# Four edits to a one-core attention and mixture-of-experts kernel: the last stores, one small sum, a weight fetch and a gate

## The chip, the core and the metric

The kernel runs on one core of one Trainium2 chip. A core has five engines that work at the same time, each through its own list of instructions in order: TensorE (PE, matrix products; its weight loads are shown as PEld), VectorE (DVE), ScalarE (ACT), GpSimd (POOL) and SyncE (SP, which here only issues transfers). Transfers run on 16 DMA engines and are issued from the lists of SP, ACT and POOL. The metric is the device time of one execution in microseconds (us). Before the change it is 377.31 us, the median of three runs (376.6 to 377.85).

## The reference: what is computed

Two stages follow each other. The first is grouped attention over 8 batches of 384 rows, with 16 query heads and 4 key/value heads of 64 columns:

```
scores = scale * np.matmul(q, k.transpose(0, 1, 3, 2))
scores = scores - np.max(scores, axis=-1, keepdims=True)
attn = np.exp(scores)
attn = attn / (np.sum(attn, axis=-1, keepdims=True) + 1e-09)
return np.matmul(attn, v)
```

Its output, 3072 rows of 1024 columns, goes through a two-level gate: softmax over 4 groups, then softmax over 4 experts of the best group. Each row goes through its one best expert and is scaled by the product of both gate weights:

```
h = np.maximum(xg[mask_e] @ w1[g, e], 0.0)
ye = h @ w2[g, e]
out[tok_idx] = combined[:, None] * ye
```

All inputs and the output are 32-bit floats. `w1` and `w2` of an expert are 1024 x 1024 each.

## The kernel before

**Staging.** The kernel works batch by batch. One attention batch has 24 units (4 key/value heads by 6 blocks of 64 keys). In unit u PE computes the scores of unit u+2 (line 308) and the product of unit u with the values (line 327), ACT takes the exponential (314), POOL adds the exponentials of two units together (`pair`, 335) and DVE sums that pair along the keys (`reduce`, 344). At the end of a batch DVE joins the partial sums (`join_keys`, 397), PE adds them over the partitions (`sums`, 405), DVE takes the reciprocal (414) and, for four parts m = 0 to 3, spreads it (421) and multiplies the attention output with it (`normalise`, 425). ACT or POOL cast the result to 16 bits (`cast`).

**Experts.** For each batch the kernel guesses one expert that its rows are likely to choose (from the mean of the values, `guess_mean`, line 446 on PE and 448 on DVE), fetches that expert's two matrices (`pick_w1`, 512, and `pick_w2`, 518, two transfers from POOL's list), and runs the expert for all rows of the batch: `moe_h` (602 on PE, ReLU on ACT at 606 and 609) and `moe_y` (616 on PE, scaling by the gate weight on ACT at 635, stores from SP at 637). A loop at the end of the program would take what no guess covered; with this input its count is zero, and the core only reads that count (916) and branches over the loop (918).

**Order.** The program is written out in the order in which each engine runs it; there is no scheduler. The expert of batch f runs in `block(f + 1)`, between the attention of batch f+1 and that of batch f+2; the expert of batch 0 runs in the last units of batch 1's attention and in `first_block`. The steps between units of batch 1 stand in the table `steps1`: an entry `22: [first_fetch]` runs after the 22nd unit's pair and reductions. `first_fetch` puts three things in POOL's list: a one-element copy that waits for the transposes of the next batch's queries (`after_transposes`, 570), and the fetches of batch 1's `w1` and `w2`. The pair of unit 23, the last, comes after it.

**Gate.** `gate_softmax` is a row of small DVE operations (471 to 491) with one exponential on ACT (497) and a few more on DVE (499 to 503); `out_weights` ends it (580, 584). Each batch's gate runs in its own block, except batch 1's: its logits come early in the attention of batch 2, and its softmax runs in `block(2)`.

**Constants.** At the start `gate_matrix_1` transposes the gate weights on PE into a PSUM tile, copies them to SBUF (233) and adds neighbouring blocks into `wgs` (236). A PE product with `wgs` follows (241).

**The last stores.** The last batch's output is made in three chunks of 128 rows by `last_y`. A chunk's 128 partitions belong to two groups of 64 rows of the output (`halves`). Chunks 0 and 1 are stored with one transfer for each group and half of the columns (904). The third chunk is made in three pieces of 512, 384 and 128 columns, and each piece is stored with one transfer that covers both groups (900): its leading dimension has 2 entries, the next one 64.

Of the kernel before, what the change touches and what calls it, by code (L numbers as in the profile page):

```python
# [18 lines left out]
def kernel(  # L19
# [11 lines left out]
    nc = tc.nc  # L31
    P = 128
    B, Hq, S, D = q.shape
    _, Hkv, _, _ = k.shape
    SC = S // P
# [190 lines left out]
    def gate_matrix_1(which):  # L226
        state["gm"] = pt = ps_tile(which, [P, 2, 512])
        pe = pt[:, 0, :Eg * 5 * KQ].rearrange("p (e n) -> p e n", e=Eg)
        wv = wraw.rearrange("a (p e) -> a e p", e=Eg)
        for e in range(Eg):  # L230
            nc.tensor.transpose(out=pe[:, e], in_=wv[:, e, :],
                                identity=id128f[:5 * KQ, :5 * KQ])
        nc.vector.tensor_copy(
            out=wg[:, :, :NW].rearrange("p k (a e) -> p e a k", e=Eg),
            in_=pe.rearrange("p e (a k) -> p e a k", k=KQ))
        nc.vector.tensor_add(out=wgs, in0=wg[:, 0::2, :NW], in1=wg[:, 1::2, :NW])

    def gate_matrix_2():
        pt = state["gm"]
# [152 lines left out]
    def join_keys(b, g0, g1):  # L392
        if b not in red:
            red[b] = gpool.tile([P, Hkv, 2, NB], F32, name="red", bufs=2)
        same = len(set(parts[b][g0:g1])) == 1
        for g, h in [(g0, g1)] if same else [(g, g + 1) for g in range(g0, g1)]:
            nc.vector.tensor_reduce(
                out=red[b][:, g:h].rearrange("p g t j -> p g (t j)"),
                in_=red3[b][:, g:h, :parts[b][g]].rearrange("p g c t j -> p g (t j) c"),
                axis=AX.X, op=ALU.add)  # L400
# [65 lines left out]
    def gate_softmax(b, gl, guessed):  # L466
        lo, hi = 0, SC + 1 if guessed else SC
        n, nt = hi, SC
        gl = gl[:, lo:hi]
        mx = gpool.tile([P, 2, SC + 1], F32, name="mx")[:, :, lo:hi]  # L470
        nc.vector.tensor_reduce(out=mx[:, 0, :], in_=gl[:, :, :G], axis=AX.X, op=ALU.max)
        sh = gpool.tile([P, 2, SC + 1, G], F32, name="sh")[:, :, lo:hi]
        nc.vector.tensor_tensor(out=sh[:, 0], in0=gl[:, :, :G],
                                in1=mx[:, 0, :].unsqueeze(2).to_broadcast([P, n, G]),
                                op=ALU.subtract)
        ohg = gpool.tile([P, SC + 1, G], F32, name="ohg")[:, lo:hi]
        nc.vector.tensor_single_scalar(ohg, sh[:, 0], 0.0, op=ALU.is_ge)
        pr = gpool.tile([P, SC + 1, G, Eg], F32, name="pr")[:, lo:hi]
        nc.vector.tensor_tensor(out=pr, in0=gl[:, :, G:NW].rearrange("p c (g e) -> p c g e", g=G),
                                in1=ohg.unsqueeze(3).to_broadcast([P, n, G, Eg]), op=ALU.mult)  # L480
        el = gpool.tile([P, SC + 1, Eg], F32, name="el")[:, lo:hi]
        nc.vector.tensor_reduce(out=el, in_=pr.rearrange("p c g e -> p c e g"), axis=AX.X,
                                op=ALU.add)
        nc.vector.tensor_reduce(out=mx[:, 1, :], in_=el, axis=AX.X, op=ALU.max)
        nc.vector.tensor_tensor(out=sh[:, 1], in0=el,
                                in1=mx[:, 1, :].unsqueeze(2).to_broadcast([P, n, Eg]),
                                op=ALU.subtract)
        ohe = gpool.tile([P, SC + 1, Eg], F32, name="ohe")[:, lo:hi]
        nc.vector.tensor_single_scalar(ohe, sh[:, 1], 0.0, op=ALU.is_ge)
        oh = oh_all[:, b, lo:hi]  # L490
        nc.vector.tensor_tensor(out=oh.rearrange("p c (g e) -> p c g e", g=G),
                                in0=ohg.unsqueeze(3).to_broadcast([P, n, G, Eg]),
                                in1=ohe.unsqueeze(2).to_broadcast([P, n, G, Eg]), op=ALU.mult)

        def weights():
            ex = gpool.tile([P, 2, SC, G], F32, name="ex")
            nc.scalar.activation(ex, sh[:, :, :nt], ACT.Exp)
            sm = gpool.tile([P, 2, SC], F32, name="smx")
            nc.vector.tensor_reduce(out=sm, in_=ex, axis=AX.X, op=ALU.add)
            wt = gpool.tile([P, SC], F32, name="wt")  # L500
            nc.vector.tensor_mul(out=wt, in0=sm[:, 0, :], in1=sm[:, 1, :])
            nc.vector.reciprocal(out=wt, in_=wt)
            nc.vector.tensor_tensor(out=cw_all[:, b], in0=oh_all[:, b, :SC],
                                    in1=wt.unsqueeze(2).to_broadcast([P, SC, NE]), op=ALU.mult)
        return weights
# [72 lines left out]
    def out_weights(b):  # L578
        m = gpool.tile([P, SC, NE], F32, name="m")
        nc.vector.tensor_tensor(out=m, in0=cw_all[:, b],  # L580
                                in1=oh1_all[:, b, :].unsqueeze(1).to_broadcast([P, SC, NE]),
                                op=ALU.mult)
        we = gpool.tile([P, SC], F32, name="we", bufs=2)
        nc.vector.tensor_reduce(out=we, in_=m, axis=AX.X, op=ALU.add)
        weff[b] = we
# [3 lines left out]
    def out_rows(o):  # L589
        return o.rearrange("(p x) d -> x p d", x=NC)  # L590

    def halves(c):

        for h in range(2):
            j = 2 * c + h
            yield slice(h * H2, (h + 1) * H2), 2 * (j % SC) + j // SC
# [26 lines left out]
    def moe_h(b, f0, which):  # L623
        if f0 == 0:
            hTs[b] = xpool.tile([P, FQ, S], BF16, name="hT", bufs=1)
        ffn_h(xb[b], w1s[b], hTs[b], f0, which)
# [97 lines left out]
    def first_fetch():  # L724
# [33 lines left out]
            do(moe_h, 0, 6, "s"),  # L758
        ],
        18: [do(before_attention, 1)],  # L760
        22: [first_fetch],
    }
    at[1].run(steps1)

# [41 lines left out]
    def block(b):  # L806
        last = b == B - 1
        f = b - 1
        if b + 2 < B:
            load_v(b + 2)  # L810
        if not last:
            after_transposes(b + 1)
        pick_w1(b)
        pick_w2(b)
        if not last:
            sum_v(b + 1)
        if b + 2 < B:
            load_k(b + 2)
            load_q(b + 2)
        moe_h(f, 0, "s")  # L820
        at[b].reduce(NU - 1)
        join_keys(b, 0, Hkv)
        moe_h(f, 2, "s")
        sums(b, 0, Hkv, "o")
        normalise(b, 0)
        normalise(b, 1)
        moe_h(f, 4, "s")
        normalise(b, 2)
        moe_h(f, 6, "s")
        cast(b, 0)  # L830
        cast(b, 1)
        if b == 2:
            gate_softmax(1, state["gl"], False)()
            out_weights(1)
        normalise(b, 3)
        moe_y(f, 0, "s")
        cast(b, 2)
        pt = ps_tile("o")
        y = ffn_y(w2s[f], hTs[f], 1, "s", (0,))
        vm = None if last else guess_mean(b + 1, pt)  # L840
        ffn_y(w2s[f], hTs[f], 1, "s", (1,), y)
        cast(b, 3)
        y_out(f, 1, y)
        gate_logits(b, pt)
        if not last:
            guess_logits(vm, guess_out(pt))
            at[b + 1] = Attn(b + 1)
            at[b + 1].score(0)
            at[b + 1].score(1)
        w = gate_softmax(b, gate_rows(pt, not last), not last)  # L850
        if not last:
            pick(b + 1)
            pick_index(b + 1)
            read_pick(b + 1)
        w()
        out_weights(b)
        y = ffn_y(w2s[f], hTs[f], 2, "o")
        if last:
            y_out(f, 2, y)
            return {}  # L860
        return {1: [do(y_out, f, 2, y, True)]}
# [25 lines left out]
    def last_y(i, c, c0, n):  # L887
        y = ps_tile("so"[i % 2])[:, 0, :n]
        for f in range(FQ):
            nc.tensor.matmul(out=y, lhsT=hTs[B - 1][:, f, c * P:(c + 1) * P],  # L890
                             rhs=w2s[B - 1][:, f, c0:c0 + n], start=(f == 0), stop=(f == FQ - 1))
        o, w = ots[c][:, c0:c0 + n], weff[B - 1][:, c:c + 1]
        if i % 2 == 0:
            nc.vector.tensor_scalar(o, y, w, None, op0=ALU.mult)
        else:
            nc.scalar.mul(o, y, w)
        rows_ = out_rows(out[(B - 1) * S:])
        if c + 1 == SC:
            xs = [x for _, x in halves(c)]
            (nc.scalar if HALF < c0 + n < DM else nc.sync).dma_start(  # L900
                out=rows_[xs[0]:xs[1] + 1:xs[1] - xs[0], :, c0:c0 + n], in_=o)
            return
        for ps, x in halves(c):
            nc.sync.dma_start(out=rows_[x][:, c0:c0 + n], in_=o[ps])

    ots = {}
    i = 0
# [107 lines left out]
```

## Time and profile before

| | us |
|---|---|
| median of three runs | 377.31 (376.6 to 377.85) |
| the profiled execution's own time | 379.33 |
| its span, from first to last instruction | 377.1 |
| PE busy | 353.9 (94%) |
| DVE, ACT, POOL busy | 245.3, 224.3, 221.5 (65%, 59%, 59%) |
| mean granted TensorE clock, as a share of full speed | 0.983 |

The profiled execution carries 2.2 us that lie outside its span. A row of the profile's views names an engine, a line, the operation, the tile it writes, an arrow and the tiles it reads; a number in square brackets at its end is the time for which the engine stood idle before it, and what released it. The lists of instructions are in order, but their times overlap between engines, so an engine's idle time costs something only where another one is waiting for it in turn. The chain of work that ended last is PE for 83% of the span; DVE follows with 6%.

### The profile page before, as it was taken

What the parts mean: (1) busy time and instruction counts of PE and PEld (TensorE: products, weight loads), DVE (VectorE), ACT (ScalarE), POOL (GpSimd) and SP (SyncE); (2) the same over time, 40 slices, a digit from 0 to 9 for tenths busy, and PEclk for the clock granted to TensorE, in tenths of its full rate; (3) what the DMA queues carried; (4) which work ended last, traced back from release to release, by engine and by line L of the source; (5) the groups of instructions that cost most, each with busy time, mean ns of one, the idle gap of its engine ahead of it and who ended that gap; (6) DMA issues with size and microseconds to landing.
All of it is one profiled execution on the core that took longest, in us unless ns stands there. A gap on an engine that the chain in (4) does not pass through costs nothing.

```text
span 377.1 us, 9174 instructions
## 1 busy us (share of the span) xinstructions
PE 353.9 (94%) x3823; PEld 185.9 (49%) x3823; DVE 245.3 (65%) x462; ACT 224.3 (59%) x296; POOL 221.5 (59%) x175
## 2 busy tenths in 40 slices
PE   7899999699999999999999999999999999999940
PEld 3445555335554555654455544654555554655520
DVE  5587669476779676857678566857678566851310
ACT  4699845259924795367925596367935596263210
POOL 8789885739963299606991199606990199300000
PEclk9999999989999999999999999999999999999995
DMA  8959999699989999999969999799959960799231
GB/s 197 203 116 166 227 170 156 117 249 250 175 157 203 233 218 196 179 207 246 192 136 209 244 199 206 135 207 248 184 107 206 247 145 2 121 205 276 56 93 37
DMA packets 69395, 67.14 MB, mean 178 GB/s; under 512 B 37054, under 2 KB 49598, under 8 KB 69350
## 3 DMA queue, kind: packets, MB, share of 16 engines
q0 software_dynamic: 26640, 41.03, 63.0%
q1 hardware_dynamic: 42228, 24.81, 29.0%
q8 instruction: 32, 0.52, 0.5%
q10 hardware_dynamic: 482, 0.67, 0.5%
q14 instruction: 13, 0.11, 0.1%
HBM read 86.07 MB, written 12.58 MB: 262 GB/s over the span
## 4 chain that ended last, share of the span: by engine, by line
PE 83%; DVE 6%; ACT 3%; POOL 2%; issue 2%; POOLq 0%; ACTq 0%
PE ps_o L327 29%; PE ps_s L602 19%; PE ps_s L616 10%; PE ps_s L308 8%; PE ps_o L616 7%; PE ps_o L440 3%; ACT e L314 2%; PE ps_s L890 1%; POOL e L335 1%; PE ps_o L405 1%; PE ps_o L602 1%; PE ps_o L890 1%; DVE xT L425 1%; DVE e L421 1%; PE ps_o L268 1%
## 5 line engine op out<-in xcount | busy, mean ns | idle before, releaser
L335 POOL TENSOR_TENSOR e<-e 128x768 f32<-128x768 f32 x91 | 162.8, 1820 | 84.9 <-PE ps_s L308 78.1
L314 ACT ACTIVATE e<-ps_s 128x768 f32<-128x768 f32 x187 | 147.4, 812 | 23.8 <-PE ps_s L308 21.4
L327 PE MATMUL ps_o<-e,v_raw 64*64 64x384 f32 x1496 | 149.1, 482 | 0.1
L344 DVE TRANSPOSE_TENSOR_REDUCE red<-e 128x24 f32<-128x768 f32 x95 | 91.5, 972 | 41.5 <-POOL e L335 41.4
L602 PE MATMUL ps_s<-xb,w 128*128 128x384 bf16 x480 | 80.9, 326 | 0.1
L327 PEld LDWEIGHTS ps_o<-e,v_raw 64*64 64x64 f32 x1496 | 54.3, 133 | 36.8 <-issue 28.9
L602 PEld LDWEIGHTS <-w 128*128 128x128 bf16 x512 | 49.5, 98 | 35.7 <-issue 4.5
L308 PE MATMUL ps_s<-qT,kT 64*64 64x384 bf16 x768 | 63.8, 326 | 1.2 <-ACT e L314 0.7
L616 PEld LDWEIGHTS <-hT 128*128 128x128 bf16 x336 | 32.2, 99 | 39.6 <-issue 3.8
L606 ACT ACTIVATE hT<-ps_s 128x768 bf16<-128x768 f32 x23 | 18.6, 810 | 55.7 <-PE ps_s L602 52.3
L616 PE MATMUL ps_s<-w,hT 128*128 128x512 bf16 x224 | 50.9, 385 | 0.0
L308 PEld LDWEIGHTS <-kT 64*64 64x64 bf16 x768 | 24.1, 105 | 36.4 <-issue 34.0
L635 ACT ACTIVATE ot<-ps_s,we 128x1024 f32<-128x1024 f32 x14 | 15.6, 1113 | 21.9 <-PE ps_s L616 20.4
L616 PE MATMUL ps_o<-w,hT 128*128 128x512 bf16 x112 | 25.6, 380 | 0.0
L369 DVE COPY xT<-ps_o 128x768 f32<-128x768 f32 x26 | 24.0, 923 | 2.0 <-PE ps_o L327 1.4
L421 DVE STREAM_TRANSPOSE e<-inv 128x768 f32<-128x768 f32 x26 | 25.2, 971 | 0.2
L425 DVE TENSOR_TENSOR xT<-xT,e 128x768 f32<-128x768 f32 x24 | 23.6, 981 | 0.8
L430 ACT CAST xb<-xT 128x768 bf16<-128x768 f32 x28 | 22.2, 833 | 0.0
L414 DVE RECIPROCAL inv<-ps_o 64x96 f32<-64x96 f32 (+2 forms) x20 | 12.7, 635 | 9.4 <-PE ps_o L405 9.2
L461 DVE STREAM_TRANSPOSE gl<-ps_o 128x96 f32<-128x96 f32 x8 | 2.3, 283 | 21.7 <-PE ps_o L453 16.1
L609 ACT ACTIVATE hT<-ps_s 128x384 bf16<-128x384 f32 x14 | 6.1, 488 | 12.5 <-PE ps_s L602 12.5
L440 PE MATMUL ps_o<-xT,wg 128*32 128x96 f32 x448 | 10.7, 248 | 0.9 <-DVE vm L448 0.9
(133 smaller groups left out, 221.5 us busy)
## 6 DMA issues: line engine op xcount, KB each, us to landing
w<-in_moe_w_dram POOLq DMA_DIRECT2D x16, 2048.0 KB, 20.7
out_dram<-ot SPq DMA_DIRECT2D x43, 256.0 KB, 6.9
q_raw<-in_q_dram POOLq DMA_DIRECT2D x7, 768.0 KB, 27.5
v_raw<-in_v_dram SPq DMA_DIRECT2D x7, 384.0 KB, 5.4
k_raw<-in_k_dram POOLq DMA_DIRECT2D x7, 192.0 KB, 24.2
out_dram<-ot SPq DMA_DIRECT2D x8, 128.0 KB, 2.4
w<-in_q_dram POOLq DMA_DIRECT2D x3, 192.0 KB, 6.6
w<-in_k_dram SPq DMA_DIRECT2D x2, 192.0 KB, 3.7
```

The costliest lines, as they stand in the source:

```text
L308: nc.tensor.matmul(out=sT[r * H2:(r + 1) * H2, s, :S], lhsT=kT[b][s * D:(s + 1) * D, key_block(b, s, g // 2, c), ks], rhs=qT[b][s * D:(s + ...
L314: nc.scalar.activation(e.rearrange("p t (s x) -> p s t x", s=2), sT[:, :, :S].rearrange("p s (t x) -> p s t x", t=2), ACT.Exp, scale=scale)
L327: nc.tensor.matmul(out=oT[t * D:(t + 1) * D, r, :S], lhsT=vraw[b][r * H2:(r + 1) * H2, g // 2, c * D:(c + 1) * D], rhs=self.e[u][r * H2:(r ...
L335: nc.gpsimd.tensor_add(out=self.e[u - 1], in0=self.e[u - 1], in1=self.e[u])
L344: nc.vector.tensor_reduce(out=red3[b][:, g, parts[b][g]].rearrange("p t j -> p (t j)"), in_=self.e[w].rearrange("p t (j x) -> p (t j) x", ...
L369: nc.vector.tensor_copy(out=dst, in_=src)
L421: nc.vector.transpose(out=rb.rearrange("p k (j x) -> p k j x", x=32), in_=inv[b][:, ks].unsqueeze(3).to_broadcast([P, 2, NB, 32]))
L425: eng.tensor_mul(out=x, in0=x, in1=rb)
L430: nc.scalar.copy(out=xb[b][:, ks, :], in_=xT[b][:, ks, :])
L440: nc.tensor.matmul(out=pt[32 * t:32 * t + 32, 0, :S // 4], lhsT=wg[:, head_pair(m), :], rhs=x[:, t], start=(m == 0), stop=(m == KQ - 1))
L602: nc.tensor.matmul(out=h[:, jj, :S], lhsT=w1[:, head_pair(m), (f0 + jj) * P:(f0 + jj + 1) * P], rhs=x[:, m, :], start=(m == 0), stop=(m == ...
L616: nc.tensor.matmul(out=y[:, nh, :], lhsT=hT[:, f, c * P:(c + 1) * P], rhs=w2[:, f, nh * HALF:(nh + 1) * HALF], start=(f == 0), stop=(f == ...
```

## The change

Four places are edited.

1. The column sum in `gate_matrix_1` reads its second operand from the PSUM tile instead of from the copy in SBUF.
2. `first_fetch` moves from step 22 of batch 1 to step 23.
3. Batch 1's `gate_softmax` and `out_weights` move, within `block(2)`, from behind the second cast to the place behind `join_keys`, before the second part of `moe_h`.
4. Each piece of the third last chunk is stored with two transfers of 64 rows. For the pieces of 384 and of 128 columns the second one is issued from ACT's list.

```diff
@@ gate_matrix_1
-        nc.vector.tensor_add(out=wgs, in0=wg[:, 0::2, :NW], in1=wg[:, 1::2, :NW])
+        nc.vector.tensor_add(out=wgs.rearrange("p g (a e) -> p g a e", e=Eg),
+                             in0=wg[:, 0::2, :NW].rearrange("p g (a e) -> p g a e", e=Eg),
+                             in1=pe.rearrange("p e (a k) -> p k a e", k=KQ)[:, 1::2])
@@ steps1
-        22: [first_fetch],
+        23: [first_fetch],
@@ block
         at[b].reduce(NU - 1)
         join_keys(b, 0, Hkv)
+        if b == 2:
+            gate_softmax(1, state["gl"], False)()
+            out_weights(1)
         moe_h(f, 2, "s")
...
         cast(b, 1)
-        if b == 2:
-            gate_softmax(1, state["gl"], False)()
-            out_weights(1)
         normalise(b, 3)
@@ last_y
-        rows_ = out_rows(out[(B - 1) * S:])
-        if c + 1 == SC:
-            xs = [x for _, x in halves(c)]
-            (nc.scalar if HALF < c0 + n < DM else nc.sync).dma_start(
-                out=rows_[xs[0]:xs[1] + 1:xs[1] - xs[0], :, c0:c0 + n], in_=o)
-            return
-        for ps, x in halves(c):
-            nc.sync.dma_start(out=rows_[x][:, c0:c0 + n], in_=o[ps])
+        engs = (nc.sync, nc.scalar) if HALF < c0 + n and c + 1 == SC else (nc.sync, nc.sync)
+        for eng, (ps, x) in zip(engs, halves(c)):
+            eng.dma_start(out=out_rows(out[(B - 1) * S:])[x][:, c0:c0 + n], in_=ots[c][ps, c0:c0 + n])
```

Line numbers of the changed kernel are 2 higher than before from the column sum on, and 3 lower behind `last_y`.

The stores at the end of SP's list before (64x512 are the two earlier chunks, the leading 2 is the pair of row groups):

```order
L904 DMA out_dram<-ot 64x512 x8
L900 DMA out_dram<-ot 2x64x512
L900 DMA out_dram<-ot 2x64x128
```

and in SP's list now:

```order
L901 DMA out_dram<-ot 64x512 x10
L901 DMA out_dram<-ot 64x384
L901 DMA out_dram<-ot 64x128
```

ACT's list ended with one store of 2x64x384; it ends now with two:

```order
L901 DMA out_dram<-ot 64x384
L901 DMA out_dram<-ot 64x128
```

Three transfers have become six, four on SP and two on ACT, and none has a leading 2.

POOL's list at the end of batch 1's attention, before (`e` are the exponentials, `tok` the one-element copy, `w_1052` and `w_1054` batch 1's expert matrices):

```order
L335 TENSOR_TENSOR e<-e 128x768 x3
L570 COPY tok<-qT 1x1
L512 ISA
L512 DMA w_1052<-in_moe_w_dram 128x8x1024
L518 ISA
L518 DMA w_1054<-in_moe_w_dram 128x8x1024
L335 TENSOR_TENSOR e<-e 128x768
L112 TENSOR_TENSOR vs<-v_raw 128x384
```

and now:

```order
L337 TENSOR_TENSOR e<-e 128x768 x4
L572 COPY tok<-qT 1x1
L514 ISA
L514 DMA w_1059<-in_moe_w_dram 128x8x1024
L520 ISA
L520 DMA w_1061<-in_moe_w_dram 128x8x1024
L112 TENSOR_TENSOR vs<-v_raw 128x384
```

The fourth pair, that of unit 23, stands ahead of the copy and the two fetches.

DVE's list in `block(2)` from the join of the key sums on, now (the first 3 and the last 2 of the 15 operations of batch 1's gate stand here; before, all 15 stood behind the third `L425`, ahead of the fourth `L421`):

```order
L399 TENSOR_REDUCE red<-red_1248 128x96
L473 TENSOR_REDUCE mx<-gl 128x3
L475 TENSOR_TENSOR sh<-gl,mx 128x12
L479 TENSOR_SCALAR ohg<-sh 128x12
...
L582 TENSOR_TENSOR m<-cw_all,oh_all 128x48
L586 TENSOR_REDUCE we<-m 128x3
L416 RECIPROCAL inv<-ps_o_1612 64x2x4x12 x2
L423 STREAM_TRANSPOSE e<-inv 128x768
L427 TENSOR_TENSOR xT<-xT,e 128x768
```

The reciprocal of batch 2's sums, and with it the whole normalising, stands behind the gate. On ACT the gate's exponential moves with it, from behind the casts to a place between the first and the second ReLU of this block.

## Rows read from the trace of the kernel before

**Rows 1.** Waits of PE: line waited for, us in total, times, longest.

```profile
PE ps_o L405 <- DVE red L397: 2.9, 1, 2.9
PE ps_o L241 <- DVE wgs L236: 1.3, 1, 1.3
PE ps_o L440 <- DVE vm L448: 0.9, 1, 0.9
```

**Rows 2.** Stretches at the end: length, busy times, then PEclk, DMA share, GB/s.

```profile
361.00:362.00 1.00, 1.00 (x8) 0.61 (x7) 0.68 (x1) 0.00 (x0) 0.00 (x0) 1.00 0.86 201
366.00:374.00 8.00, 0.00 (x0) 0.00 (x0) 0.00 (x0) 0.00 (x0) 0.00 (x0) 0.61 0.13 50
```

**Rows 3.** Stores of lines 904 and 900: ns min/median/max to issue, first and last start.

```profile
L904 SPq DMA_DIRECT2D out_dram<-ot x8: 466/534/591, 355.1 to 360.4; - x8
DMA to landing us min/median/max: 2.2/2.4/2.4
...
L900 SPq DMA_DIRECT2D out_dram<-ot x2: 518/570/622, 361.7 to 363.0; - x2
```

**Rows 4.** Line 918, the branch at the end, same columns.

```profile
L918 SPq EVENT_SEMAPHORE  x9: 17/17/17, 364.1 to 375.4; - x9
...
L918 ACTq EVENT_SEMAPHORE  x1: 17/17/17, 366.3 to 366.3; - x1
```

**Rows 5.** Order of time, 9 to 28 us: start, us, engine, line, operation.

```profile
9.84 1.81 POOL L335 TENSOR_TENSOR e<-e 128x768 f32<-128x768 f32 x1
10.13 1.61 DVE L236 TENSOR_TENSOR wgs<-wg 128x80 f32<-128x80 f32 x1
...
25.67 0.95 DVE L425 TENSOR_TENSOR w<-w,ps_o 128x768 f32<-128x768 f32 x1
25.80 1.83 POOL L335 TENSOR_TENSOR e<-e 128x768 f32<-128x768 f32 x1 [0.52 <-PE ps_s L308]
```

**Rows 6.** Order of time, end of batch 1's attention, 60 to 75 us.

```profile
61.56 5.39 POOL L335 TENSOR_TENSOR e<-e 128x768 f32<-128x768 f32 x3 [4.40 <-PE ps_s L602]
62.28 3.06 ACT L314 ACTIVATE e<-ps_s 128x768 f32<-128x768 f32 x4
66.29 5.35 PE L616 MATMUL ps_s<-w,hT 128*128 128x512 bf16 x24
68.59 0.18 POOL L570 COPY tok<-qT 1x1 bf16<-1x1 bf16 x1 [1.64 <-DMA qT<-q_raw]
...
70.99 1.82 POOL L335 TENSOR_TENSOR e<-e 128x768 f32<-128x768 f32 x1
72.84 0.98 DVE L344 TRANSPOSE_TENSOR_REDUCE red<-e 128x24 f32<-128x768 f32 x1 [4.30 <-POOL e L335]
```

**Rows 7.** The chain that ended last, 74 to 81 us: start, us, what.

```profile
74.57 1.17 PE ps_o L405 x4
75.74 2.76 PE ps_s L616 x8
78.50 1.73 PE ps_o L616 x8
```

**Rows 8.** One stretch, columns as in rows 2.

```profile
74.50:76.00 1.50, 1.43 (x6) 1.14 (x7) 0.24 (x2) 0.00 (x0) 1.44 (x3) 0.50 0.92 171
```

**Rows 9.** Order of time, block 2, 108 to 122 us.

```profile
110.08 0.18 POOL L570 COPY tok<-qT 1x1 bf16<-1x1 bf16 x1 [2.74 <-DMA qT<-q_raw]
110.26 1.52 DVE L414 RECIPROCAL inv<-ps_o 64x96 f32<-64x96 f32 x2 [1.40 <-PE ps_o L405]
...
114.74 0.45 POOL L114 TENSOR_TENSOR vsum<-vs 128x128 bf16<-128x128 f32 x1
...
118.02 0.16 DVE L471 TENSOR_REDUCE mx<-gl 128x3 f32<-128x12 f32 x1
...
120.44 0.17 PE L446 MATMUL ps_o<-halfb,vsum 128*128 128x2 bf16 x1
...
121.09 0.97 DVE L421 STREAM_TRANSPOSE e<-inv 128x768 f32<-128x768 f32 x1
```

## What was predicted

> **What bounds the kernel now.** I read the chain of waits first: PE holds 83% of it, and from 132 us on it is almost unbroken PE work. Next I read PE's own waits. Only three of them touch the edits: 2.9, 1.3 and 0.9 us [rows 1]. The rest of PE's time is work that this change neither adds nor removes, so the first three edits can be worth little more than these waits and what hangs on them. Then I read the end of the span, which no PE wait shows. The last matmul ends at 362.59 and the last arithmetic at 362.96, yet the span ends at 377.1, so 14 us pass in which no engine computes. The view by stretches shows what goes on there: from 366 to 374 the DMA engines move a steady 50 GB/s at a busy share of 0.13 [rows 2], which is two engines of 16. SP's semaphore waits at line 918 run until 375.4 [rows 4], just after that traffic stops; from there it is 1.7 us to the end of the span.
>
> **Part 1, the last stores.** Before the change these are three stores, each with a leading dimension of 2, of 256, 192 and 64 KB, together 0.52 MB. At 50 GB/s that is 10.5 us. The first is issued at 361.7 [rows 3]; with some 2.4 us from issue to landing the traffic would run from 364 to 374.6: the rate alone accounts for the wait until 375.4. The eight stores of line 904, with 64 leading rows, run otherwise: while they were being moved the share was 0.86 and the rate 201 GB/s, and each landed 2.4 us after its issue [rows 2, 3]. The six new stores have the same 64 leading rows.
>
> The Trainium skill (DMA: Bandwidth & Descriptors, section "Why a DMA increments its semaphore by 16 and not by 1") says that a transfer uses the largest number of engines, up to 16, that divides the size of the slowest dimension that is not 1; that would be 2 for the old stores and 16 for the new ones. The trace agrees with the first, 0.13 of 16, and the stores of line 904 fit the second. The same page (section "Rules for kernel authors") speaks against this change: it advises against two transfers to disjoint partition halves, since both go over the same 16 engines, and says that issuing from several engines saves only issue time. By that rule alone part 1 would be worth nothing; it is the first rival below. The row with 0.13 speaks against it, because here the single transfer did not go over 16.
>
> Worked out: SP issues its four stores at about 0.55 us each [rows 3], the first at 361.7, then one by one as the pieces are ready; the last waits for the arithmetic that ends at 362.96 (the old last store was issued at 363.0 [rows 3]) and for the third, and is issued at 363.4. It lands at 363.4 + 2.4 = 365.8. ACT issues one store more than before, 0.55 us; its last semaphore at line 918 came at 366.3 [rows 4] and now comes at 366.85. That is later than the landing, so ACT ends the kernel: 366.85 + 1.7 = 368.55, 8.55 us less than 377.1. Bounds: if what ACT did before 366.3 was itself slowed by the old stores, the landing decides, 367.5, or 9.6 less. If six stores at once land in twice 2.4 us, it is 368.2 + 1.7 = 369.9, or 7.2 less. I take 8.55, since both its numbers are rows.
>
> **Part 2, the column sum.** The sum of 80 columns took 1.61 us, from 10.13 to 11.74, and POOL's pair, begun at 9.84, ended at 11.65 [rows 5]: the sum ended with it. A DVE product of 768 columns with one operand in PSUM, at 25.67, took 0.95 us though POOL ran a pair from 25.80 on [rows 5]. So two operands in SBUF wait for POOL here, and one in PSUM doesn't. With one in PSUM I put 80 columns at 0.25 us (estimate: a tenth of 0.95 and an overhead), which ends at 10.4. PE is busy until 10.54, so its 1.3 us wait [rows 1] is gone: 1.25 us. Up to 61 us PE and ACT follow each other with no wait on a transfer in the chain, so I carry it all. Bounds: 0, if the sum still waits for POOL or a transfer eats it, and 1.3.
>
> **Part 3, the fetch behind the last pair.** POOL ends unit 21's pair at 66.95 [rows 6]. It then waits for the transposes, copies at 68.59, issues two fetches and only at 70.99 begins unit 23's pair, whose exponential ACT had finished at 65.34. DVE had stood idle for 4.30 us when the pair came, and PE waited 2.9 us for the sums. In the new order the pair runs at 66.95 to 68.8, inside POOL's wait for the transposes. The copy follows at 68.8, 0.2 us later than before, and so do the fetches; a weight fetch lands 20.7 us after its issue (the page's median), about 90, and PE wants it after batch 2's attention, near 100, so this costs nothing. DVE is done with reduction and join at 70.5, while PE is busy with 24 products until 71.64: the 2.93 us wait is gone and 1.1 us of slack stands in its place.
>
> More hangs on it. After that wait the granted clock was 0.50, the lower level of 1.2 GHz [rows 8]. The sums took 1.17 us and eight products 2.76, where the next eight, from 78.50 on, took 1.73 again [rows 7]. Without the wait PE does not stop, and I take full speed: 0.59 and 1.03 us more, 4.55 together. DVE's normalising and the casts on ACT follow the sums but not those eight products, so they come only 2.93 + 0.59 = 3.5 us earlier, and early in batch 2 PE waits for ACT, which scales and stores the expert's output behind those casts. Between 3.5 and 4.55 I take 4.1. If the clock falls all the same, it is 2.9.
>
> **Part 4, the gate ahead of the sums.** The 15 operations took 3.07 us (118.02 to 121.09) and stood between the third and the fourth normalising step [rows 9]. PE waited 0.9 us behind them [rows 1]. Now they start when the join ends, at 110.26 - 1.40 = 108.86 in old times. DVE was idle for those 1.40 us, waiting for the sums, so the gate fills that and delays the reciprocal by 1.7, not 3.1. The fourth step ends 1.4 us earlier; of that about half a microsecond may go, since after part 3 POOL's pairs, and so the join, gain less than PE does. PE's wait shrinks from 0.94 to some 0.15: 0.8 us, between 0 and 0.94. The gate's exponential now stands ahead of the second ReLU on ACT, which it delays by some 0.8 us; PE wants that ReLU's PSUM tile again only two groups of 16 products (2.6 us each) later, so the delay is hidden. If it were not, PE would lose those 0.8 us.
>
> **Sum.** 8.55 + 1.25 + 4.1 + 0.8 = 14.7 us. The profiled execution, 379.33 with 2.2 outside its span, would come to 364.6, its span to 362.4. The median of the runs lies 2.0 below the profiled execution; the parts lie in device work that both contain, so I take them from the median: 377.31 - 14.7 = 362.6.
>
> **Rivals.**
> *The halves gain nothing.* Both halves share the engines and the end stays where it was: 377.31 - 6.15 = 371.2. For it: only the rule above. Against it: 0.13 against 0.86.
> *The transfers take the middle back.* In block 2 POOL's copy already waited 2.74 us for the next queries' transposes, at 110.08, and the sum of the values was done at 115.19, 5.2 us before PE used it [rows 9]. The loads behind this are nearly continuous, so they do not move with PE. After parts 2 and 3 PE comes there 5.3 us earlier, at about 115.1, and stands right on that edge; with part 2's gain the fetches start about a microsecond earlier as well, which just covers it. If the loads do not move and land 3 us later because they collide with other traffic, PE stops there and 4 of the 6.15 us are lost, the clock included: 366.6.
> *One edit of the two small ones is eaten*, part 2 behind POOL or part 4 behind the join: 363.4 to 363.9.
> *Slower.* The gate's exponential on ACT waits for DVE, which waits for the join. If DVE comes late, the second and later ReLUs are late, PE stands idle in block 2, and the clock falls as it did after the 2.93 us wait. [...]
>
> **How the numbers follow.** Forecast 0.68, one small edit eaten 0.13, the middle taken back 0.11, halves gain nothing 0.06, slower 0.01, and 0.01 for no change at all. The range takes in the bounds: all gains at their best (9.6 + 1.3 + 4.55 + 0.94 = 16.4) give 360.9, and with the spread of the runs (0.6) 360.2; at their worst with one small edit eaten (7.2 + 0 + 2.9 + 0.4) they give 366.8, which covers the middle taken back too. I say 360.0 to 367.2. About 0.3% of the time, 1.1 us, is what a measurement can tell from no change. Every case but two lies more than 5 us below the time before: faster 0.97, same 0.02, slower 0.01.
>
> **What would show it.** After the last matmul the DMA share should be high for 3 us and then 0, with no stretch at 0.13, and the span should end 6 us after that matmul, not 14.5. The column sum should last under 0.4 us, with no PE wait at the product with `wgs`. The sums of batch 1 should follow the 24 products with no wait, at a granted clock of 1.00 throughout. PE's wait of 0.9 us ahead of the gate's products in block 2 should be under 0.3, and from batch 3 on each block should run as before, only earlier. The prediction is wrong if two-engine traffic remains at the end, if PE's wait for the sums of batch 1 only moves to another tile, or if a new PE wait of over 1 us stands in block 2.

## The result, and the profile after

The changed kernel took 363.59 us (median; 362.76 to 363.79, 4 runs), the kernel before 376.96 (376.08 to 377.85, 4 runs): a ratio of 0.9641 [0.9612, 0.967], 13.4 us less. Another six runs of it gave 363.53 (363.27 to 363.90) against 376.87 for the kernel before, 0.9648 [0.9611, 0.9685]. The forecast was 362.6, its range 360.0 to 367.2. The profiled execution took 363.79, 361.2 of them in the span. Here and below, ratios are formed without single runs that took over 1.5% more than the fastest run of the same kernel; ranges and medians take in all runs.

First PE's waits, which answer to [rows 1]: line waited for, us in total, times, longest. These are the first five.

```profile
PE ps_o L270 <- DVE onesb L162: 1.6, 1, 1.6
PE ps_s L310 <- ACT e L316: 0.7, 1, 0.7
PE ps_o L448 <- ACT ot L637: 0.3, 1, 0.3
PE ps_s L310 <- ACT qT L257: 0.2, 1, 0.2
PE ps_o L407 <- ACT w L369: 0.2, 1, 0.2
```

The waits for `red`, `wgs` and `vm` are all gone from the head of the list.

The end of the span by stretches, for [rows 2]: stretch, length, busy us of PE, PEld, DVE, ACT and POOL, then granted clock, DMA share, GB/s.

```profile
354.50:355.50 1.00, 1.00 (x8) 0.59 (x6) 0.71 (x1) 0.00 (x0) 0.00 (x0) 1.00 0.83 195
355.50:357.00 1.50, 0.61 (x10) 0.43 (x7) 0.35 (x1) 0.58 (x1) 0.00 (x0) 1.00 0.60 135
357.00:359.50 2.50, 0.00 (x0) 0.00 (x0) 0.00 (x0) 0.00 (x0) 0.00 (x0) 0.84 0.70 172
359.50:361.00 1.50, 0.00 (x0) 0.00 (x0) 0.00 (x0) 0.00 (x0) 0.00 (x0) 0.50 0.00 0
```

The last matmul ends at 356.13. The stores behind it now move at 0.70 of the 16 engines and 172 GB/s where they moved at 0.13 and 50, and at 359.5 the traffic is over. The span ends 5.07 us after the last matmul; before it was 14.5.

What issues and ends these stores, for [rows 3, 4]: engine's queue, operation, count, ns min/median/max, first and last start.

```profile
L901 SPq DMA_DIRECT2D out_dram<-ot x12: 466/567/988, 348.7 to 357.5; - x12
L901 ACTq DMA_DIRECT2D out_dram<-ot x2: 545/554/563, 356.4 to 357.0; - x2
DMA to landing us min/median/max: 2.0/2.4/3.0
```

```profile
L913 ACTq TENSOR_LOAD <-left_i x1: 1016/1016/1016, 357.6 to 357.6; - x1
...
L915 SPq EVENT_SEMAPHORE  x9: 17/17/17, 358.6 to 359.5; - x9
...
L915 ACTq EVENT_SEMAPHORE  x1: 17/17/17, 358.9 to 358.9; - x1
```

ACT's last event (358.9) is ahead of SP's (359.5), which is the landing of the last store: 357.5 + 2.0. From there it is 1.7 us to the end, as before.

The start, for [rows 5], in order of time: start, us, engine, line, operation.

```profile
9.61 1.81 POOL L337 TENSOR_TENSOR e<-e 128x768 f32<-128x768 f32 x1
...
10.41 0.24 DVE L236 TENSOR_TENSOR wgs<-wg,ps_o 128x80 f32<-128x80 f32 x1
10.75 0.45 PE L243 MATMUL ps_o<-wgs,mod 128*128 128x80 f32 x2
```

The column sum lies inside POOL's operation and takes 0.24 us where it took 1.61; PE's product follows with no wait.

The end of batch 1's attention, for [rows 6, 7], same view:

```profile
60.48 7.17 POOL L337 TENSOR_TENSOR e<-e 128x768 f32<-128x768 f32 x4 [4.40 <-PE ps_s L604]
65.21 5.35 PE L618 MATMUL ps_s<-w,hT 128*128 128x512 bf16 x24
67.58 0.18 POOL L572 COPY tok<-qT 1x1 bf16<-1x1 bf16 x1
67.68 0.98 DVE L346 TRANSPOSE_TENSOR_REDUCE red<-e 128x24 f32<-128x768 f32 x1 [0.23 <-POOL e L337]
...
69.63 1.01 POOL L112 TENSOR_TENSOR vs<-v_raw 128x384 f32<-128x384 f32 x1
70.40 0.58 PE L407 MATMUL ps_o<-red,half 128*128 128x96 f32 x4
70.73 0.45 POOL L113 TENSOR_TENSOR vs<-vs 128x128 f32<-128x128 f32 x1
70.82 1.89 PE L618 MATMUL ps_s<-w,hT 128*128 128x512 bf16 x8
```

POOL's pairs are now four in a row, and its copy waits for nothing. DVE's reduction waits 0.23 us, not 4.30. The sums follow the 24 products at once; they take 0.58 us and the eight products 1.89. Before, the same view had 1.17 and 2.97:

```profile
74.57 1.17 PE L405 MATMUL ps_o<-red,half 128*128 128x96 f32 x4 [2.93 <-DVE red L397]
75.53 2.97 PE L616 MATMUL ps_s<-w,hT 128*128 128x512 bf16 x8
```

The stretch that answers to [rows 8]:

```profile
70.40:74.40 4.00, 4.00 (x25) 1.92 (x26) 3.30 (x4) 1.11 (x1) 2.79 (x5) 1.00 1.03 167
```

PE has work for all of it, at a granted clock of 1.00 (2.4 GHz).

Block 2, for [rows 9]:

```profile
103.96 0.15 DVE L473 TENSOR_REDUCE mx<-gl 128x3 f32<-128x12 f32 x1
...
106.90 0.20 DVE L586 TENSOR_REDUCE we<-m 128x3 f32<-128x48 f32 x1
107.03 1.51 DVE L416 RECIPROCAL inv<-ps_o 64x96 f32<-64x96 f32 x2
107.65 0.18 POOL L572 COPY tok<-qT 1x1 bf16<-1x1 bf16 x1 [5.14 <-DMA qT<-q_raw]
...
113.03 0.45 POOL L114 TENSOR_TENSOR vsum<-vs 128x128 bf16<-128x128 f32 x1
...
114.99 0.17 PE L448 MATMUL ps_o<-halfb,vsum 128*128 128x2 bf16 x1
```

The gate's chain runs ahead of the reciprocal. POOL's copy comes 2.4 us earlier than it did (110.08), so the loads moved some way with PE; the sum of the values is done at 113.48, and PE uses it at 114.99.

### The profile page after: what moved, and what is told of

It reads as the page before. It is cut to its first block, busy times and chain, and to the rows that moved or that the text cites. A ratio compares the mean times of both kernels' runs of the same rounds, so it can differ in the third digit from the quotient of the medians.

```text
span 361.2 us, 9178 instructions
## 1 busy us (share of the span) xinstructions
PE 352.7 (98%) x3823; PEld 185.0 (51%) x3823; DVE 244.3 (68%) x462; ACT 224.6 (62%) x296; POOL 222.8 (62%) x175
## 4 chain that ended last, share of the span: by engine, by line
PE 90%; ACT 3%; DVE 3%; POOL 1%; issue 1%; POOLq 0%; ACTq 0%
PE ps_o L329 31%; PE ps_s L604 20%; PE ps_s L618 13%; PE ps_s L310 9%; PE ps_o L618 6%; PE ps_o L442 3%; ACT e L316 2%; PE ps_s L892 2%; PE ps_o L604 1%; PE ps_o L407 1%; PE ps_o L892 1%; PE ps_o L270 1%; POOL e L337 1%; DVE ps_o L423 1%; DVE red L346 1%
## 5 line engine op out<-in xcount | busy, mean ns | idle before, releaser
L618 PE MATMUL ps_s<-w,hT 128*128 128x512 bf16 x224 | 49.8, 379 | 0.0
L442 PEld LDWEIGHTS ps_o<-xT,wg 128*32 128x32 f32 x448 | 9.2, 110 | 3.1 <-issue 2.7
```

The costliest lines, as they stand in the source:

```text
L442: nc.tensor.matmul(out=pt[32 * t:32 * t + 32, 0, :S // 4], lhsT=wg[:, head_pair(m), :], rhs=x[:, t], start=(m == 0), stop=(m == KQ - 1))
L618: nc.tensor.matmul(out=y[:, nh, :], lhsT=hT[:, f, c * P:(c + 1) * P], rhs=w2[:, f, nh * HALF:(nh + 1) * HALF], start=(f == 0), stop=(f == ...
```

## The experiments

Twelve more kernels ran, two of them repeats of the kernel before and of the changed one. Times are medians.

**Each part alone** (on the kernel before). The edit is that part of the change's diff and nothing else; of each, only the lines that tell it apart stand here:

```diff
# stores alone
+engs = (nc.sync, nc.scalar) if HALF < c0 + n and c + 1 == SC else (nc.sync, nc.sync)
...
# column sum alone
...
+in1=pe.rearrange("p e (a k) -> p k a e", k=KQ)[:, 1::2])
# fetch alone
-22: [first_fetch],
+23: [first_fetch],
# gate alone: the two calls behind `if b == 2:` ahead of moe_h(f, 2, "s")
```

The last stores alone:

> The kernel before with part 1 alone (six stores of 64 rows at the end). Prediction's theory: 8.55 us less than before, about 368.4 against 376.96. Rival, the halves gain nothing: 376 to 378. The traces of before and after differ by 9.4 us behind the last matmul (14.5 against 5.1) while the medians of the whole change differ by 13.4, not by the 15.9 of the spans: if the missing 2.5 us lie in this part, it measures about 7, or 370.

The column sum alone:

> The kernel before with part 2 alone (column sum with one operand in PSUM). Prediction's theory: the sum lasts 0.25 us, PE's wait of 1.3 us at the product with wgs is gone, 1.25 us less than before, about 375.7. Rival, a later wait takes it back: the sum is short in the trace all the same, but PE's wait for the sums of batch 1 grows from 2.9 to 4.2 us or the wait in block 2 grows, and the time is that of before, 376.5 to 377.4.

The fetch alone:

> The kernel before with part 3 alone (fetches of batch 1 behind the last pair). Prediction's theory: 4.1 us less than before, about 372.9, with no wait at the sums of batch 1 and a granted clock of 1.00 from 70 to 80 us. If the clock falls all the same: 2.9 us, 374.1. Rival, the middle takes it back because the transfers do not move: PE waits in block 2 for the sum of the values or the transposes and 1 us or less is left, 376.

The gate alone:

> The kernel before with part 4 alone (batch 1's gate ahead of the sums). Prediction's theory: PE's 0.94 us wait in block 2 is gone, 0.8 to 0.94 us less than before, about 376.1. Rival, the reciprocal comes 1.7 us later and the wait stays: no difference, 376.5 to 377.4.

Measured, beside 377.38 for the kernel before (374.72 to 380.80, 29 runs):

| kernel | us (range, runs) | ratio [95%] | by the ratio, us |
|---|---|---|---|
| stores alone | 369.27 (367.37 to 371.54, 6) | 0.9789 [0.975, 0.9829] | -8.0 |
| column sum alone | 376.55 (374.86 to 377.25, 12) | 0.9975 [0.9947, 1.0003] | -0.9 |
| fetch alone | 374.69 (373.49 to 376.82, 12) | 0.9945 [0.9916, 0.9973] | -2.1 |
| gate alone | 378.11 (373.63 to 379.33, 12) | 1.0009 [0.9972, 1.0046] | +0.3 |

The four sum to 10.7 us with wide intervals (the kernel before spreads over 6 us), so only the first and the third are resolved here. In the profiles all four do what they say: the tail of the span falls to 5.13 us with the stores alone and stays at 14.5 in the other three; PE's wait for `wgs` is gone with the sum alone; the sums of batch 1 have no wait with the fetch alone; with the gate alone PE's wait for `vm` is 0.29. The 0.9 of [rows 1] is no fixed number to set beside that: in six profiles with the gate in its old place this wait is 0.4 to 1.2 us, in eight with the new place 0 to 0.3.

**The kernel before once more**, unedited, for a second profile:

> The kernel before, unchanged, with a profile of its own. If the first profile (379.33, span 377.1, clock 0.983) was an ordinary execution, this one has the same span within 0.5 us and the same 14.5 us behind the last matmul. If that execution was longer than the median by some 2.4 us, this one shows which stretch was longer: the tail (then 12 us instead of 14.5), or PE's part before it (then the last matmul ends near 360 instead of 362.6).

It took 376.74 (374.76 to 379.60, 12 runs; ratio 0.9971 [0.9937, 1.0004]): the same kernel beside itself is as far from 1 as the column sum alone was. The last matmul ends at 359.95, 2.6 us earlier than in the first profile (362.59), and the tail is again 14.5. So the first profile is of an execution with a long PE part, and the difference arises at the sums of batch 1: the 24 products ahead of them start 0.2 us apart in the two profiles (66.29 and 66.08), the eight behind them end 3.2 us apart (78.50 and 75.30). The two rows there in this second profile:

```profile
67.37 0.18 POOL L570 COPY tok<-qT 1x1 bf16<-1x1 bf16 x1
...
72.89 0.69 PE L405 MATMUL ps_o<-red,half 128*128 128x96 f32 x4 [1.45 <-DVE red L397]
```

The copy did not wait for the transposes at all; PE's wait was 1.45 us, not 2.93, the sums took 0.69 us, not 1.17, and the eight products 1.89, not 2.97.

**One part undone** (from the changed kernel). The fetch:

```diff
-23: [first_fetch],
+22: [first_fetch],
```

> The changed kernel with part 3 undone (fetches of batch 1 ahead of the last pair, parts 1, 2 and 4 kept). Prediction's size: 4.1 us more than the changed kernel, 367.7, in every run. The other reading: PE's wait at the sums of batch 1 is 1.5 us in some runs and up to 2.9 in others, and only in the latter the granted clock falls; then the median is 2 to 3 us above the changed kernel, about 366, and the runs spread over 3 us or more.

It took 366.72 (364.55 to 368.88, 6 runs) beside 363.53 for the changed kernel: 3.2 us more, with no overlap of the ranges; the six runs lie 1.0 to 5.4 us above it, so 4.1 is not ruled out by them. The wait is back. In order of time:

```profile
66.20 0.18 POOL L572 COPY tok<-qT 1x1 bf16<-1x1 bf16 x1 [0.34 <-DMA qT<-q_raw]
...
68.61 1.83 POOL L337 TENSOR_TENSOR e<-e 128x768 f32<-128x768 f32 x1
...
72.20 0.69 PE L407 MATMUL ps_o<-red,half 128*128 128x96 f32 x4 [1.66 <-DVE red L399]
```

The spread is back too: 4.3 us over six runs, against 0.6 and 1.0 in the two sets of the changed kernel.

The gate behind the casts again:

```diff
+if b == 2:                       # behind cast(b, 1), not ahead of moe_h(f, 2, "s")
+    gate_softmax(1, state["gl"], False)()
+    out_weights(1)
```

> The changed kernel with part 4 undone (batch 1's gate behind the second cast, parts 1 to 3 kept). Prediction's theory: PE's wait ahead of the gate's products in block 2 is back with 0.9 to 1.1 us, and the kernel is 0.8 to 1.0 us slower than the changed one, about 364.5. Rival: the wait is back but hidden later, 0 to 0.3 us.

It took 364.44 (364.13 to 364.55, 6 runs), 0.9 more than the changed kernel, with no overlap. Its wait at the gate's products of block 2 is a little shorter than expected:

```profile
117.61 1.53 PE L442 MATMUL ps_o<-xT,wg 128*32 128x96 f32 x64 [0.74 <-DVE vm L450]
```

In the changed kernel these products start with no wait of PE, at 116.84.

**Both operands in SBUF, but POOL idle.** The column sum as before the change, and POOL's first pair moved behind the second, so that POOL has nothing to do while the sum runs:

```diff
+nc.vector.tensor_add(out=wgs, in0=wg[:, 0::2, :NW], in1=wg[:, 1::2, :NW])
+0: Attn(0, act_copies=(0, 1, 3), later=(1,),
+3: [do(at[0].pair, 1)],
```

> The changed kernel with part 2 undone (both operands of the column sum in SBUF) and POOL's first pair moved behind the second one in POOL's list, so that POOL has no pair to run at 10 us. If the long sum was DVE waiting for POOL, it lasts 0.3 us or less here too, PE doesn't wait, and the time is that of the changed kernel within 0.5 us. If two operands in SBUF are slow by themselves in this form, it lasts 1.6 us, PE waits 1.3 and the time is about 364.8.

It took 363.68 (363.42 to 363.89, 6 runs), the time of the changed kernel. In order of time:

```profile
10.45 0.24 DVE L236 TENSOR_TENSOR wgs<-wg 128x80 f32<-128x80 f32 x1
...
12.37 1.82 POOL L335 TENSOR_TENSOR e<-e 128x768 f32<-128x768 f32 x1 [2.38 <-PE ps_o L327]
```

The same sum with the same operands as in [rows 5] takes 0.24 us once POOL is idle. So its 1.61 us were DVE waiting out POOL's operation, and one operand in PSUM is one of two ways past it. The five profiles with the old sum beside POOL's first pair say the same: it lasted 0.98 to 1.76 us, according to when the pair began, and ended 0.1 us behind that pair each time. That the whole kernel took the same time is partly luck: PE has a new wait of 0.79 us that ends at 18.34 (for DVE's copy of the transposed keys, `kT`), the spans are 0.7 us longer than those of the changed kernel (middle of six 361.95 and 361.25), and 1.65 to 1.81 us lie outside them instead of 2.13 to 2.60.

**All last stores from SP**, still in halves of 64 rows:

```diff
-engs = (nc.sync, nc.scalar) if HALF < c0 + n and c + 1 == SC else (nc.sync, nc.sync)
+engs = (nc.sync, nc.sync)
```

> The changed kernel with all six stores of the last chunk on SP, none on ACT. If the number of engines that a store uses is all that part 1 changes, SP issues two stores more, 1.1 us, and ACT two fewer: the last store starts about 1.1 us later, so 0.5 to 1.1 us slower than the changed kernel, about 364.4. If the second queue is what made the gain, it loses most of the 9 us: 370 or more.

It took 365.66 (364.91 to 366.33, 6 runs; ratio to before 0.9667 [0.9634, 0.97]), 2.1 us more than the changed kernel, where 0.5 to 1.1 were expected. This kernel and the next two ran on another chip than the changed one, where the kernel before took 378.23 (17 runs) instead of 376.87; by the ratios the difference is 0.7 to 1.0 us and not resolved. The spans are clearer: 362.7 to 363.7 us here, 361.0 to 362.0 in the next kernel on the same chip, 361.1 to 361.7 in the changed one. The issues and the last events:

```profile
L901 SPq DMA_DIRECT2D out_dram<-ot x14: 466/587/821, 348.5 to 358.4; - x14
```

```profile
L915 SPq EVENT_SEMAPHORE  x9: 17/17/17, 359.6 to 361.3; - x9
...
L915 ACTq EVENT_SEMAPHORE  x1: 17/17/17, 356.3 to 356.3; - x1
```

The last issue comes 0.9 us later than in the changed kernel and the last landing 1.8 us later; the two-queue part of the edit is worth this, and the shape of the stores the rest. Issue time is only half of the 1.8 us; the other half is one landing: the trace's semaphore records have fifteen of the last store's sixteen landings by 360.34, 0.8 us behind the changed kernel's last (359.51), and the sixteenth at 361.26. What held that one is not shown.

**Every last store in both queues**, the first piece too:

```diff
+engs = (nc.sync, nc.scalar) if c + 1 == SC else (nc.sync, nc.sync)
```

> The changed kernel with the second half of every piece of the last chunk on ACT, so three stores on each queue. SP's last store then starts about 0.5 us earlier, but ACT's last one starts no earlier than before (357.0) and its landing ends the kernel: 0 to 0.5 us less than the changed kernel, 363.1 to 363.6. If issuing on ACT delays its scaling of the 384 columns by a store's 0.55 us: up to 0.5 us more, 364.1.

363.26 (363.13 to 364.16, 6 runs): not to be told from the changed kernel. ACT issues three stores, and SP's last event comes at 360.3 in the profile, which is of the slowest of the six; no gain from more issue in parallel shows.

**The first of the three pieces as one transfer** with a leading dimension of 2, the other two in halves:

```diff
+if c + 1 == SC and c0 == 0:
+    xs = [x for _, x in halves(c)]
+    nc.sync.dma_start(out=out_rows(out[(B - 1) * S:])[xs[0]:xs[1] + 1:xs[1] - xs[0], :, :n], in_=o)
+    return
```

> The changed kernel with the first piece of the last chunk (512 columns, 256 KB) stored by one transfer with a leading dimension of 2, as before the change; the other two pieces as in the changed kernel. If such a transfer uses two engines at 50 GB/s together, it needs 5.2 us from about 2.4 us after its issue at 355.2, so it lands at 362.8 and the kernel ends 3.3 us later than the changed one, about 366.9; the trace shows a share of 0.13 for about 4 us. If the number of transfers or queues mattered and not the leading dimension, it is within 0.6 us of the changed kernel, since SP then issues one store fewer.

368.14 (367.98 to 368.65, 6 runs; ratio 0.9734 [0.9702, 0.9767]), 4.6 us more than the changed kernel, where 3.3 were expected. Its end by stretches, columns as above:

```profile
357.00:358.00 1.00, 0.00 (x0) 0.00 (x0) 0.00 (x0) 0.00 (x0) 0.00 (x0) 1.00 0.12 31
358.00:359.00 1.00, 0.00 (x0) 0.00 (x0) 0.00 (x0) 0.00 (x0) 0.00 (x0) 1.00 0.39 38
359.00:360.00 1.00, 0.00 (x0) 0.00 (x0) 0.00 (x0) 0.00 (x0) 0.00 (x0) 1.00 0.83 191
360.00:361.00 1.00, 0.00 (x0) 0.00 (x0) 0.00 (x0) 0.00 (x0) 0.00 (x0) 1.00 0.56 148
361.00:362.00 1.00, 0.00 (x0) 0.00 (x0) 0.00 (x0) 0.00 (x0) 0.00 (x0) 0.61 0.17 48
362.00:363.00 1.00, 0.00 (x0) 0.00 (x0) 0.00 (x0) 0.00 (x0) 0.00 (x0) 0.50 0.13 49
```

One such transfer is enough to bring the stretch at 0.13 and 49 GB/s back. SP's last event falls at 364.3, 4.8 us later than in the changed kernel. The 3.3 counted the large store alone, at 50 GB/s from 357.6 on. It landed at 363.8 instead of 362.8, since the first two microseconds moved less than that, and the stores issued behind it landed later still: of the sixteen landings of SP's store of 384 columns fourteen had come by 360.51, the two others at 363.87 and 364.04 (semaphore records of the trace).

**The changed kernel once more**, to stand beside those with one part undone:

> The changed kernel, unchanged, as the measure for the next three on the same chip. Its runs should lie within 1.5 us of each other, around 363.5, where those of the kernel before spread over 5 us: if part 3 takes away a wait that differs from run to run, the spread goes with it.

363.53, as told above; the tail and the waits are as in the first profile of it. No version ran that is faster than the changed kernel by more than the measurement can tell.

## Why the prediction was right, point by point

The time came out 1.0 us above the forecast. The sum of 14.7 stands against 13.4 measured. (The chances of its four faster cases add up to 0.98, not the 0.97 that I gave.) Its terms:

| term | predicted (bounds) | alone | undone |
|---|---|---|---|
| 1 last stores | 8.55 (7.2 to 9.6) | 8.0 (6.4 to 9.4) | not run |
| 2 column sum | 1.25 (0 to 1.3) | 0.9 (-0.1 to 2.0) | not run |
| 3 fetch | 4.1 (2.9 to 4.55) | 2.1 (1.0 to 3.2) | 3.2 |
| 4 gate | 0.8 (0 to 0.94) | not resolved | 0.9 |

**Last stores.** The mechanism held. In the spans the tail, from the last matmul to the end, shows it without the spread of the rest:

| kernel | last matmul ends | span | tail |
|---|---|---|---|
| before | 362.59 | 377.1 | 14.5 |
| before, second profile | 359.95 | 374.5 | 14.5 |
| stores alone | 363.75 | 368.9 | 5.13 |
| changed | 356.13 | 361.2 | 5.07 |
| all from SP | 355.92 | 363.0 | 7.04 |
| first piece as one | 356.31 | 366.0 | 9.68 |

That is 9.4 us in the span, more than the 8.55 that I took and just under the upper bound, for the reason that this bound named: what ACT did ahead of its last event was itself longer with the old stores. Its register read behind its store, in the kernel before:

```profile
L916 ACTq TENSOR_LOAD <-left_i x1: 2517/2517/2517, 363.5 to 363.5; - x1
```

It took 2516 ns in the second profile of before and takes 1016 in the changed kernel. I had carried ACT's 366.3 over and added an issue; ACT was done at 358.9 instead, and the landing decides. Some 0.3 us of the 9.4 are given back outside the span. The record has time and span of every run: with the old stores 1.71 to 2.31 us lie outside it (104 runs, middle one 1.88), with the new stores alone 2.10 to 2.64 (6 runs, 2.19), in the changed kernel 2.13 to 2.71 (10 runs). Why is not shown, and the stores alone do not settle it: with POOL's first pair moved as well it was 1.65 to 1.81.

The semaphore records of the trace agree with two engines before and sixteen now: each of the six new stores ends with sixteen landings; the old one of 256 KB has one rise at 362.71 and then two landings, at 371.27 and 371.29, 9.6 us after its issue.

The first rival, that the halves gain nothing, did not hold: with all stores on one queue the tail is 7.5 us shorter than before (14.5 - 7.04), and the second queue adds 2.0. The rule beside it, in the Trainium skill (DMA: Bandwidth & Descriptors, section "Rules for kernel authors"), that halves of the partitions are not worth two transfers, is not what this kernel shows, because here the single transfer ran on two engines; what it says of several issuing engines, that they save issue time only, agrees with the last issue that came 0.9 us later from SP alone, and with fifteen of that store's sixteen landings, but not with the 2.0 us of the tail, of which the late sixteenth landing makes about half.

**Column sum.** Its place, its cause (POOL) and its 0.24 us (0.25 forecast) are shown. What it is worth in the whole is not resolved: 0.9 us alone, in an interval that holds 0. Its 1.25 us, too, were one execution's: PE's wait for `wgs` is 0.6 to 1.4 us in five profiles with the old sum.

**Fetch: the term that was mis-sized.** The order of things is as predicted, and the wait is gone with nothing late in its place. But 4.1 us were read from one execution, and PE's wait there is not the same in each. It is 1.3 us plus what POOL's copy waits for the transposes (1.45 where the copy waits for nothing), as six profiles with the old order show:

| kernel | copy waits | PE waits at the sums | granted clock behind it |
|---|---|---|---|
| before | 1.64 | 2.93 | 0.50 |
| stores alone | 1.43 | 2.73 | 0.50 |
| gate alone | 1.24 | 2.54 | 1.00 |
| sum alone | 0.94 | 2.26 | 0.50 |
| fetch undone | 0.34 | 1.66 | 1.00 |
| before, second profile | 0 | 1.45 | 1.00 |

The wait of 2.93 that I took is the longest of these, and the fall of the clock behind it, which I took as given, came in three of the six. Two of the rows behind the last column (stretch, length, busy times, then granted clock, share, GB/s), first of the sum alone, then of the gate alone:

```profile
72.70:74.20 1.50, 1.50 (x6) 1.21 (x7) 0.34 (x1) 0.00 (x0) 1.44 (x3) 0.50 1.10 157
```

```profile
73.60:75.10 1.50, 1.48 (x9) 1.01 (x10) 0.75 (x1) 0.00 (x0) 1.44 (x3) 1.00 1.05 160
```

In time, the last matmul ends 6.5 us earlier than in the first profile of before (6.15 forecast for parts 2 to 4), but 3.8 earlier than in the second. So the typical worth lies between the wait without the clock and my 4.1; the runs say 2.1 and 3.2. A fault in method stands behind it: the three waits of PE were taken from an execution 2 us above the median and then subtracted from the median. That the total still came out within 1.0 us is partly luck: a term of the fetch that was too large stood beside one of the stores that was 0.9 us too small in the span.

**Gate.** 0.8 forecast and 0.9 measured by undoing it; the gate alone showed the wait at 0.29 but not the time, in a kernel that spreads over 5.7 us.

**The rivals.** The middle was not taken back: POOL's copy moved 2.4 us earlier with PE, and the sum of the values was done 1.5 us ahead of its use, a thinner margin than the 5.2 us before [rows 9]. No small edit was eaten as far as the rows show. Nothing is slower: in block 2 PE is busy for 26.92 of 27 us at a granted clock of 1.00 (columns as in the stretches above):

```profile
103.00:130.00 27.00, 26.92 (x282) 14.08 (x283) 21.97 (x57) 16.50 (x23) 13.24 (x12) 1.00 1.01 204
```

**Left open.** What makes the transposes of batch 2's queries land at different times, and what changed the time outside the span. The kernel with the fetch alone, whose sums have no wait, still spreads over 3.3 us, and that goes with the clock: its three runs at a mean granted clock of 0.981 took 376.3 to 376.8, the nine at 0.984 to 0.988 took 373.5 to 375.3. Where the clock fell in those three is not known; the one that was profiled is not among them.

## What to carry to other kernels

Look at what lies behind the last matmul first: a DMA share of 0.13 there is two engines of 16, and it came from the leading dimension of the transfer, not from its bytes, so cutting the transfer where that dimension becomes 64 gained 7.5 us of the tail, and a second queue 2.0 more. A wait that ends with a transfer has a size for each execution; before it is priced, read it from two or more, because it also adds to the spread: bringing it back into the changed kernel raised that from 0.6 to 4.3 us. An edit that takes under 1 us off can be resolved by undoing it from a kernel without such a wait, and not by making it in one that has it.

## What the runs showed of the hardware that was not expected

- The clock's fall is not told by the length of PE's wait alone: it was at 0.50 behind a wait of 2.26 us and stayed at 1.00 behind one of 2.54.
- ACT's read of a register from SBUF took 2.48 to 2.52 us in five profiles where it stood right behind a two-engine store on ACT's own queue, and 0.47 to 1.11 us in nine without that (0.47 with no store on ACT, 1.05 with the two-engine store on SP).
- A single two-engine store delays the 64-row stores issued after it: with the first piece as one transfer the stretch from 357 to 359 ran at 31 to 38 GB/s, the next store's last two landings came at 363.9 and 364.0, over 3 us behind its other fourteen, and the kernel lost 4.6 us.
- DVE's sum waited for POOL; beside DVE's products POOL's operations were longer, too. In block 2 of the changed kernel DVE's product at 109.59 took 1.16 us, and POOL's operation beside it 1.54, where it took 1.01 at 69.63. The next product, at 111.68, took 0.96, and POOL's operation begun with it 1.26, where it took 0.45 at 70.73. In order of time:

```profile
109.59 1.16 DVE L427 TENSOR_TENSOR xT<-xT,e 128x768 f32<-128x768 f32 x1
110.07 1.54 POOL L112 TENSOR_TENSOR vs<-v_raw 128x384 f32<-128x384 f32 x1
...
111.68 0.96 DVE L427 TENSOR_TENSOR xT<-xT,e 128x768 f32<-128x768 f32 x1
111.69 1.26 POOL L113 TENSOR_TENSOR vs<-vs 128x128 f32<-128x128 f32 x1
```
